# A gated linear attention and a maxout feed-forward in one kernel: where the loads of spans 5 to 9 and three stores stand in SyncE's queue

## The chip, the cores and the metric

The kernel runs on one core of one Trainium2 chip. The metric is the device time of one execution in microseconds (us); lower is better. The engines are TensorE (PE, with its weight loads as PEld), VectorE (DVE), ScalarE (ACT), GpSimd (POOL) and SyncE (SP). In this kernel SP does nothing but issue DMA transfers.

## What is computed

Inputs are `q`, `k`, `v` and `f_logit`, each 4 x 8 x 768 x 48 (batch, head, position, head dimension), and three weight matrices, all in float32. The first part is a gated recurrence for each batch and head:

```python
f = 1.0 / (1.0 + np.exp(-f_logit))
for t in range(S):
    state = f[:, :, t, :, None] * state + np.einsum('bhd,bhe->bhde', k[:, :, t], v[:, :, t])
    y[:, :, t] = np.einsum('bhd,bhde->bhe', q[:, :, t], state)
```

The second part takes the result as 3072 tokens of 384 values and puts them through a feed-forward of width 1024:

```python
h1 = x @ w1
h2 = x @ w2
g = np.maximum(h1, h2)
return (g @ w_out).astype(np.float32)
```

The output is 3072 x 384 in float32.

## The kernel before

**Tiling.** A *span* is 256 positions of one batch with all eight heads. There are 12 spans, numbered so that span s is window s // 4 of batch s % 4: spans 0 to 3 are the first windows of the four batches, spans 4 to 7 the second, spans 8 to 11 the third. The state that span s leaves is what span s + 4 begins with. Within a span two neighbouring positions share a partition, so that a tensor of a span is 128 partitions x 768 values, 384 KB.

**An order written out by hand.** The scheduler is switched off (`tc.manual_schedule()`). The string `ORDER` is a list of words, and the loop at the end of the kernel runs one step for each word. Each engine does its own steps in the order of the words; between engines only data dependencies count (and one added rule, below). A word has a letter for the step, the span (and sometimes a part), a letter for the engine (`a` ACT, `v` DVE, `p` POOL, `s` SP) and, behind `@`, a slot or a PSUM bank. The words that matter here:

- `Lf6@12`, `Lq`, `Lk`, `Lv`: SP loads one tensor of span 6 into slot 12 of `slots`, 27 slots of 384 KB in SBUF (line 126, `load`). A slot is used again later, so a load may have to wait for the last reader of what lay there. Slots 0 to 11 first hold the raw weights, 12 to 15 an intermediate of the weights.
- `E`, `F`, `G` (ACT): the gate from `f`, its logarithm, and one factor from that. `e` (DVE or POOL) adds two neighbouring positions, `C` (PE) sums over positions, `X` and `Z` (ACT) are the exponentials of the sums.
- `i` (POOL or DVE, line 248) multiplies `k` by a factor, in place in the slot; `j` (DVE, line 252) does the same to `q`. `K` (line 259) and `Q` (line 262) scale them into the tiles `kp` and `qp`, and `V` casts `v` into `vb`.
- `t` and `u` (PE, line 276) transpose `kp` and `qp` into PSUM, `U` copies the result to SBUF (`trs`).
- `A` (PE, line 293) forms the products of positions, `m` (DVE, line 300) masks them, `D` (PE, line 388) forms what a span adds to the state, `n` and `N` update the state. `S` and `y` (PE, lines 315 and 324) add up the attention output; `z` (DVE, lines 356 and 358) reads a column of the output's banks between the two halves `S.0` and `S.1`, so that the second half waits for it.
- `Y` copies the output to SBUF. For spans 6 to 10 it goes on through `M` (SP, line 428), a DMA transpose; for those spans the tile `xr` between `Y` and `M` has one buffer.
- `d` (PE, line 437) multiplies by `w1 - w2`, `r` takes the positive part, `o` (PE, line 462) multiplies by `w_out` and by the product `w2 @ w_out`, which together give the maximum. `b` copies an output block to `ob`, which has three buffers (spans 0, 3, 6, 9 share one, and so on), and `O` (SP, line 483 for most spans) stores it to HBM.

The feed-forward of a span stands some spans behind its attention in the list, so that PE has matrix products of `d` and `o` between the short steps of the attention.

**An added rule.** A POOL step among `e`, `i`, `K`, `Q`, `V`, `N` and some of the weights' steps also waits for the DVE step of that set that stands last before it in the list:

```python
        if key in SHARED and e in ("v", "p"):
            ins = nc.cur_bb.bb.instructions[-1]
            if e == "v":
                ahead = ins.name
            elif ahead:
                tc.add_manual_dep(ins, ahead, ...
```

**SP's queue.** SP issues one transfer after the other. A transfer whose slot is not free, or whose `ob` is not written, holds up all that stand behind it. Eight semaphores serve the transfers in turn, so that a transfer also waits for the one eight places ahead of it.

Of the kernel before, what the change touches and what calls it, by code (L numbers as in the profile page):

```python
# [17 lines left out]


ORDER = """  # L20
Lf0s@16 g0v Lf1s@17 Lq0s@18 Lk0s@19 Lk1s@20 Lv0s@21 Lq1s@22 Wa2s E0 Wb1s F0 Lv1s@23 E1 e0v C0@0 F1
Wb2s j0v Z0 e1v X0 Q0v G0 C1@1 Wb0s i0v X1 u0@2 G1 g2v K0v Lf2s@24 i1p t0@2 U0.0v@2 U0.1a@3 Wa0s V0v
Z1 K1v D0@2 A0.1@0 Wa3s j1v A0.0@4 Q1v Wa1s m0.1v@0 u1@6 t1@6 Wo0s n0.0v U1.0a@6 U1.1a@7 Wo1s V1v
n0.1v D1@0 m0.0v@4 S0.0@2 A1.0@6 Lk2s@25 wc2a z0v@2 m1.0v@6 A1.1@4 S0.1 y0 Lq2s@26 wc0a ws2p n1.0v
n1.1v m1.1v@4 S1.0@6 Y0.0a@2 wt2@0 Lf3s@16 E2 g5p z1v@6 N1.1v S1.1 y1 N0.1p Lv2s@17 g3p ws0v wt0@1
Y1.1a@7 wx2a@0 Y0.1v@3 wc1p Lq3s@18 Y1.0v@6 d0.2@2 F2 g1p ws3v d0.0@4 Lk3s@19 wx0a@1 wt1@0 g4v e2v
d0.3@3 ws1v C2@1 r0.1a@2 d1.2@6 Lf4s@21 wo0v wx1v@0 wo1p d0.1@5 G2 d1.3@7 r0.0v@4 d1.0@2 Lv3s@20
wo2p wo3a d1.1@3 r1.1v@6 Z2 wm0@0 X2 g6v Lk4s@22 r1.0a@2 i2v wm1@1 K2v Lf5s@23 j2v wm2@2 Q2v Lq4s@24
E3 wn1v@1 t2@4 u2@4 F3 U2.0v@4 Lf6s@12 V2p wn2a@2 wn0v@0 o0.1@1 U2.1v@5 e3p A2.1@2 Lq5s@13 b0.1.0a@1
D2@4 A2.0@6 G3 n2.0v C3@0 j3v o1.1@1 Z3 n2.1v Lk5s@0 i3v X3 Q3v o1.0@0 m2.1v@2 E4 K3p F4 m2.0v@6  # L30
b1.1.0a@1 S2.0@2 V3p u3@4 z2v@2 t3@4 e4p S2.1 y2 U3.2v@4 D3@6 Y2.2a@2 C4@1 n3.0v N2.1v A3.0@4 G4
n3.1v A3.1@2 m3.0v@4 E5 o0.0@6 i4p F5 m3.1v@2 Z4 d2.2@4 X4 e5v G5 j4v S3.0@2 b0.0.0a@6 d2.3@5 K4v E6
O0.2s C5@1 Lq6s@1 d2.1@7 z3v@2 r2.1a@4 Q4v Lv4s@2 S3.1 y3 Lk6s@3 F6 j5v Lf7s@4 N3.1v t4@4 X5 Y3.2v@2
i5p u4@4 Lv6s@5 Z5 d2.0@6 U4.2v@4 e6p d3.1@3 r2.0a@6 d3.0@2 g7p K5v G6 C6@1 d3.2@4 r3.0a@2 Q5v
d3.3@5 Z6 j6v X6 t5@2 u5@2 Q6v r3.1a@4 o2.1@1 U5.2v@2 V4a i6p b1.0.0a@0 O1.2s A4.1@2 K6p D4@4
m4.1v@2 A4.0@6 Lv5s@6 E7 o3.1@0 Lf8s@7 F7 Lq7s@8 n4.0v m4.0v@6 Lf9s@9 N4.0p e7p Lq9s@10 t6@2
b3.1.0a@0 u6@2 Lk7s@11 n4.1v G7 A5.0@6 U6.2v@2 S4.0@4 b2.1.0a@1 o3.0@0 m5.0v@6 V5p C7@1 z4v@4
b3.0.0v@0 A5.1@2 X7 A6.0@6 S4.1 y4 m5.1v@2 Z7 E8 D5@0 Y4.2v@4 V6a o2.0@2 F8 m6.0v@6 d4.2@4 n5.0v
b2.0.0a@2 N5.0v G8 d4.3@5 O2.2s n5.1v j7v Lq8s@25 S5.0@0 r4.1a@4 A6.1@2 N4.1v Lf11s@26 D6@6 z5v@0
Q7p S5.1 y5 Lv7s@14 n6.0v E9 m6.1v@2 Lk8s@15 d4.0@4 Y5.2a@0 Lv8s@16 d4.1@5 e8p Lf10s@17 F9 Lv9s@18  # L40
d5.1@1 r4.0v@4 i7p Lk9s@21 d5.0@0 o4.1@2 j8v r5.0a@0 N6.0v K7v n6.1v C8@3 e9v d5.2@0 Z8 b4.1.0v@2 G9
S6.0@4 u7@6 X8 t7@6 z6v@4 j9v S6.1 y6 V7v d5.3@1 U7.2v@6 i8p o4.0@2 r5.1a@0 Y6.2v@4 Q8p E11 M6s
A7.0@0 b4.0.0v@2 A7.1@4 D7@6 N5.1p m7.0v@0 o5.0@3 Lq11s@19 K8p Lk11s@20 n7.0v O3.2s m7.1v@4 C9@2
N7.0p b5.0.0a@3 t8@0 Z9 u8@0 N6.1v S7.0@4 V8v X9 o5.1@3 U8.2v@0 V9a F11 n7.1v i9v D8@2 b5.1.0a@3
A8.1@0 z7v@4 N7.1p A8.0@6 n8.0v E10 m8.1v@0 d6.2@2 K9p d6.3@3 m8.0v@6 d6.0@0 r6.1a@2 N8.0p d6.1@1
Q9v S8.0@2 r6.0a@0 S7.1 y7 z8v@2 j11v t9@6 u9@6 e11v Y7.2a@4 S8.1 y8 U9.2v@6 C11@0 G11 M7s o6.1@1
F10 i11p Z11 Lk10s@23 X11 Q11p o6.0@4 Y8.2a@2 e10p A9.0@6 b6.0.0a@4 D9@0 M8s A9.1@2 K11p n9.0v
d7.1@5 m9.1v@2 C10@0 O5.2s d7.0@4 Z10 m9.0v@6 Lq10s@22 b6.1.0a@1 d7.3@3 Lv11s@12 G10 d7.2@2 O4.2s
r7.0a@4 N9.0v i10p Lv10s@24 d8.3@7 O6.2s X10 d8.1@5 r7.1a@2 K10v d8.2@6 d8.0@4 r8.1a@6 o7.1@1
r8.0a@4 j10v Q10p S9.0@2 t11@4 t10@6 z9v@2 u11@4 S9.1 y9 U11.0v@4 u10@6 U11.1v@5 o7.0@0 U10.2a@6  # L50
V11v V10v b7.1.0v@1 o8.1@4 Y9.2a@2 b7.0.0a@0 M9s D10@1 b8.1.0a@4 D11@0 O7.2s A11.0@2 A10.0@6 n11.0v
A11.1@4 m10.0v@6 o8.0@0 m11.1v@4 d9.0@6 N11.0v n10.0v d9.1@7 m11.0v@2 N10.0p d9.3@5 r9.0a@6 d9.2@4
b8.0.0v@0 O8.2s S10.0@0 r9.1a@4 S11.0@2 z10v@0 A10.1@6 z11v@2 S11.1 y11 m10.1v@6 S10.1 y10 Y11.0a@2
Y11.1a@3 o9.0@4 Y10.2a@0 M10s d11.2@5 b9.0.0v@4 d11.1@0 d11.3@1 o9.1@4 d10.1@3 b9.1.0v@4 r11.4a@5
d10.0@2 O9.2s d10.2@4 r10.0a@2 d10.3@5 d11.0@2 r10.1v@4 o10.0@3 r11.2a@2 r11.3v@0 r11.5v@1 o10.1@0
b10.0.0a@3 o11.0@1 b10.1.0v@0 O10.2s o11.1@0 b11.0.0v@1 O11.0s o11.2@1 b11.1.1a@0 O11.1s b11.1.2a@1
O11.2s
"""


# [523 lines left out]
```

## Time and profile before

| | |
|---|---|
| three runs | 139.15, 140.23, 140.26 us, median 140.23 us |
| the profiled execution's own time | 141.28 us |
| its span, first to last instruction | 139.5 us |
| loaded from and stored to HBM in it | 23.59 MB and 4.72 MB |
| DMA of under 512 bytes a packet | 54368 of 59768 packets |
| one load of 384 KB, issue to landing, median | 6.1 to 6.5 us |
| one store of 384 KB, issue to landing, median | 4.6 us |

The profile tells the busy time of each engine, which engine or transfer ended each idle time, and when each transfer was issued and had landed. A matmul is pipelined, so that its shown duration includes time in which the next one already runs: the start of a group against the start of the next one tells how long PE had it. A wait for several things is put down to the one that came last, and where the engine that is named had long been done, it was another, often a DMA.

### The profile page before, as it was taken

Reading aid. Unit: us, or ns where it says so; the run is one execution under the profiler, and the core shown is the slowest. Engines: PE = TensorE matmul, PEld = TensorE weight load, DVE = VectorE, ACT = ScalarE, POOL = GpSimd, SP = SyncE. Lnnn points to the kernel's source line nnn. Section 1 sums busy time; section 2 is a strip of 40 time slices with the busy share of each in tenths; the row PEclk is TensorE's granted clock in tenths of the full one; section 3 lists DMA queues with packets and bytes.
Section 4 is the critical chain, followed back from the end, with each engine's and each line's share of the span. In section 5 each row is a group of like instructions: output and inputs, shape, how many; then the busy total and the mean of one; then the engine's idle time right before and its main releaser. Section 6 shows DMA issues by size and latency. Waiting matters only on the chain. (4 is left out here: it accounts for less than half of the span.)

```text
span 139.5 us, 5553 instructions
## 1 busy us (share of the span) xinstructions
PE 119.7 (86%) x2455; PEld 89.9 (64%) x2455; DVE 100.9 (72%) x173; ACT 79.0 (57%) x120; POOL 43.6 (31%) x52
## 2 busy tenths in 40 slices
PE   0044489699999989999999899989989999999991
PEld 0024378586567678667787666766877668778671
DVE  5688798999889989979985989981742768312630
ACT  3684257865583979853884356695565814504301
POOL 5002008540509206094055095629525001000000
PEclk9999999999999999999999999999999999999999
DMA  4999999999999889999999999909699061422124
GB/s 104 271 261 294 344 339 348 370 272 246 270 264 241 222 234 260 251 303 244 247 265 262 224 275 180 297 5 146 170 257 329 16 140 34 117 56 60 58 61 165
DMA packets 59768, 29.65 MB, mean 213 GB/s; under 512 B 54368, under 2 KB 58592, under 8 KB 59744
## 3 DMA queue, kind: packets, MB, share of 16 engines
q1 hardware_dynamic: 59744, 29.30, 85.0%
q8 instruction: 19, 0.31, 1.0%
q14 instruction: 5, 0.04, 0.1%
HBM read 23.59 MB, written 4.72 MB: 203 GB/s over the span
## 5 line engine op out<-in xcount | busy, mean ns | idle before, releaser
L437 PE MATMUL banks<-xT,wd 128*128 128x256 bf16 x288 | 34.6, 273 | 1.6 <-DVE xT L115 1.1
L462 PE MATMUL banks<-wo,gT 128*128 128x384 bf16 (+1 forms) x200 | 35.3, 320 | 0.0
L437 PEld LDWEIGHTS <-wd 128*128 128x128 bf16 x288 | 27.2, 98 | 6.0 <-POOL state L180 1.2
L446 ACT ACTIVATE gT<-banks 128x1024 bf16<-128x1024 f32 (+1 forms) x20 | 19.5, 981 | 18.2 <-PE banks L437 13.6
L300 DVE TENSOR_TENSOR at_m<-banks,mask 128x1024 bf16<-128x1024 f32 x24 | 28.8, 1216 | 0.8 <-PE banks L293 0.5
L462 PEld LDWEIGHTS <-gT 128*128 128x128 bf16 x200 | 19.2, 98 | 11.8
L248 POOL TENSOR_TENSOR slots<-slots,one 128x384 f32<-128x384 f32 x8 | 8.0, 999 | 29.5 <-DVE kp L259 8.6
L462 PE MATMUL banks<-m,xT 128*128 128x384 bf16 (+1 forms) x75 | 15.9, 320 | 0.0
L214 ACT ACTIVATE gate<-slots 128x768 f32<-128x768 f32 x12 | 10.1, 841 | 7.0 <-DMA slots<-in_f_logit_dram 6.0
L115 ACT COPY ob<-banks 128x384 f32<-128x384 f32 (+1 forms) x16 | 7.3, 457 | 11.8 <-PE banks L462 11.8
L115 DVE COPY trs<-banks 128x2048 bf16<-128x2048 bf16 (+1 forms) x12 | 11.9, 996 | 2.5 <-PE banks L276 2.5
L115 DVE COPY ob<-banks 128x384 f32<-128x384 f32 x9 | 5.0, 554 | 8.9 <-PE banks L462 8.9
L229 PE MATMUL banks<-e,u_inc 128*128 128x384 bf16 x12 | 4.2, 353 | 8.2 <-DVE e L225 8.1
L405 DVE TENSOR_TENSOR tmp_s<-banks,state 128x192 f32<-128x192 f32 x16 | 5.6, 352 | 7.0 <-PE banks L388 6.4
L218 ACT ACTIVATE ell<-gate 128x768 f32<-128x768 f32 x12 | 10.2, 847 | 0.2
L259 POOL TENSOR_TENSOR kp<-slots,inv 128x768 bf16<-128x768 f32 x5 | 9.1, 1817 | 3.8 <-DVE qp L262 3.7
L293 PE MATMUL banks<-trs 48*64 48x128 bf16 x384 | 10.1, 234 | 0.2
L262 POOL TENSOR_TENSOR qp<-slots,dec 128x768 bf16<-128x768 f32 x4 | 7.3, 1814 | 8.9 <-PE banks L388 6.2
L252 DVE SCALAR_TENSOR_TENSOR slots<-gate,slots 128x384 f32<-128x384 f32 x12 | 6.6, 551 | 3.0 <-DMA slots<-in_q_dram 3.0
L115 ACT COPY trs<-banks 128x1024 bf16<-128x1024 bf16 (+1 forms) x4 | 4.8, 1227 | 7.0 <-PE banks L276 7.0
L293 PEld LDWEIGHTS <-trs 48*64 48x64 bf16 x384 | 7.5, 115 | 1.7 <-issue 1.1
L462 PEld LDWEIGHTS <-xT 128*128 128x128 bf16 x75 | 6.5, 97 | 3.2
(73 smaller groups left out, 185.9 us busy)
## 6 DMA issues: line engine op xcount, KB each, us to landing
slots<-in_f_logit_dram SPq DMA_DIRECT2D x12, 384.0 KB, 6.5
slots<-in_q_dram SPq DMA_DIRECT2D x12, 384.0 KB, 6.1
slots<-in_k_dram SPq DMA_DIRECT2D x12, 384.0 KB, 6.3
slots<-in_v_dram SPq DMA_DIRECT2D x12, 384.0 KB, 6.1
out_dram<-ob SPq DMA_DIRECT2D x6, 384.0 KB, 4.6
out_dram<-ob SPq DMA_DIRECT2D x11, 192.0 KB, 3.5
slots<-in_moe_w_dram SPq DMA_DIRECT2D x4, 384.0 KB, 8.7
slots<-in_moe_w_dram SPq DMA_DIRECT2D x3, 512.0 KB, 8.7
```

Source lines behind the costliest of these rows:

```text
L115: (nc.scalar.copy if e == "a" else engines[e].tensor_copy)(out, in_)
L214: nc.scalar.activation(flat(gate[s]), flat(loaded[s]["f"]), AF.Exp, bias=0.0, scale=-1.0)
L218: nc.scalar.activation(flat(ell[s]), flat(gate[s]), AF.Ln, bias=1.0, scale=1.0)
L248: engines[e].tensor_mul(even, even, one[s])
L252: engines[e].scalar_tensor_tensor(out=even, in0=gate[s][:, :, 1, :], scalar=1.0, in1=even, op0=ALU.add, op1=ALU.mult)
L259: engines[e].tensor_mul(pad("kp", s)[:, :, :, 0:D], by_parity(loaded[s]["k"]), both(inv[s]))
L262: engines[e].tensor_mul(pad("qp", s)[:, :, :, 0:D], by_parity(loaded[s]["q"]), both(dec[s][:, 0:HD].rearrange("p (h d) -> p h d", h=H)))
L293: nc.tensor.matmul(out=ps[h * HC:(h + 1) * HC, j % 2, par, :], lhsT=t[rows, h, 0, j, par, :], rhs=t[rows, h, 1, j].rearrange("p a t -> p ( ...
L300: nc.vector.tensor_mul(at[s][:, jj].rearrange("p r j a t -> p (r j) (a t)"), banks[:, b:b + 2, :].rearrange("p r (j x) -> p (r j) x", j=2) ...
L437: nc.tensor.matmul(out=ps[:, f], lhsT=wd[:, kt, ff * C:(ff + 1) * C], rhs=xT[g][:, kt], start=(kt == 0), stop=(kt == KT - 1))
L446: nc.scalar.activation(dst, src, AF.Relu)
L462: nc.tensor.matmul(out=ps, lhsT=lhs, rhs=rhs, start=(i == 0), stop=(i == len(terms) - 1))
```

## The change

Only the string `ORDER` changes. All words are kept, with their slots and banks, and all words that are not for SP stand in the same order as before. On SP 17 words take other places among the transfers 32 to 49 (counted from 0). The lists of SP in that stretch, before and after; the transfers ahead of them and behind them are the same:

```diff
 Lk5@0
-O0.2 Lq6@1 Lv4@2 Lk6@3 Lf7@4 Lv6@5 O1.2 Lv5@6 Lf8@7
-Lq7@8 Lf9@9 Lq9@10 Lk7@11 O2.2 Lq8@25 Lf11@26 Lv7@14 Lk8@15
+Lq6@1 Lv4@2 Lk6@3 Lf7@4 O0.2 Lv5@6 Lf8@7 Lv6@5 Lq7@8
+O1.2 Lf9@9 Lk7@11 Lq8@25 Lv7@14 Lq9@10 Lk8@15 O2.2 Lf11@26
 Lv8@16
```

`O0.2` goes behind four loads, `O1.2` behind three others (`Lv5`, `Lf8`, `Lq7`), and `O2.2` behind `Lq8`, `Lv7` and `Lk8`. Among the loads, `Lv6` goes behind `Lv5` and `Lf8`; `Lk7`, `Lq8` and `Lv7` go ahead of `Lq9`; `Lv7` and `Lk8` go ahead of `Lf11`. From `Lv8` on every transfer has its old place.

More of the change, by code (lines that the diff above doesn't have):

```diff
@@ L20 @@
 ORDER = """
[L21 to L54, printed above, removed]
@@ L55 @@
-d10.0@2 O9.2s d10.2@4 r10.0a@2 d10.3@5 d11.0@2 r10.1v@4 o10.0@3 r11.2a@2 r11.3v@0 r11.5v@1 o10.1@0
-b10.0.0a@3 o11.0@1 b10.1.0v@0 O10.2s o11.1@0 b11.0.0v@1 O11.0s o11.2@1 b11.1.1a@0 O11.1s b11.1.2a@1
-O11.2s
+Lf0s@16 g0v Lf1s@17 Lq0s@18 Lk0s@19 Lk1s@20 Lv0s@21 Lq1s@22 Wa2s E0 Wb1s F0 Lv1s@23 E1 e0v C0@0 F1 Wb2s
+j0v Z0 e1v X0 Q0v G0 C1@1 Wb0s i0v X1 u0@2 G1 g2v K0v Lf2s@24 i1p t0@2 U0.0v@2 U0.1a@3 Wa0s V0v Z1 K1v
+D0@2 A0.1@0 Wa3s j1v A0.0@4 Q1v Wa1s m0.1v@0 u1@6 t1@6 Wo0s n0.0v U1.0a@6 U1.1a@7 Wo1s V1v n0.1v D1@0
@@ new lines @@
+m0.0v@4 S0.0@2 A1.0@6 Lk2s@25 wc2a z0v@2 m1.0v@6 A1.1@4 S0.1 y0 Lq2s@26 wc0a ws2p n1.0v n1.1v m1.1v@4
+S1.0@6 Y0.0a@2 wt2@0 Lf3s@16 E2 g5p z1v@6 N1.1v S1.1 y1 N0.1p Lv2s@17 g3p ws0v wt0@1 Y1.1a@7 wx2a@0
+Y0.1v@3 wc1p Lq3s@18 Y1.0v@6 d0.2@2 F2 g1p ws3v d0.0@4 Lk3s@19 wx0a@1 wt1@0 g4v e2v d0.3@3 ws1v C2@1
+r0.1a@2 d1.2@6 Lf4s@21 wo0v wx1v@0 wo1p d0.1@5 G2 d1.3@7 r0.0v@4 d1.0@2 Lv3s@20 wo2p wo3a d1.1@3 r1.1v@6
+Z2 wm0@0 X2 g6v Lk4s@22 r1.0a@2 i2v wm1@1 K2v Lf5s@23 j2v wm2@2 Q2v Lq4s@24 E3 wn1v@1 t2@4 u2@4 F3
@@ new lines @@
+U2.0v@4 Lf6s@12 V2p wn2a@2 wn0v@0 o0.1@1 U2.1v@5 e3p A2.1@2 Lq5s@13 b0.1.0a@1 D2@4 A2.0@6 G3 n2.0v C3@0
+j3v o1.1@1 Z3 n2.1v Lk5s@0 i3v X3 Q3v o1.0@0 m2.1v@2 E4 K3p F4 m2.0v@6 b1.1.0a@1 S2.0@2 V3p u3@4 z2v@2
+t3@4 e4p S2.1 y2 U3.2v@4 D3@6 Y2.2a@2 C4@1 n3.0v N2.1v A3.0@4 G4 n3.1v A3.1@2 m3.0v@4 E5 o0.0@6 i4p F5
+m3.1v@2 Z4 d2.2@4 X4 e5v G5 j4v S3.0@2 b0.0.0a@6 d2.3@5 K4v E6 C5@1 Lq6s@1 d2.1@7 z3v@2 r2.1a@4 Q4v
+Lv4s@2 S3.1 y3 Lk6s@3 F6 j5v Lf7s@4 O0.2s N3.1v t4@4 X5 Y3.2v@2 i5p u4@4 Z5 d2.0@6 U4.2v@4 e6p d3.1@3
@@ new lines @@
+r2.0a@6 d3.0@2 g7p K5v G6 C6@1 d3.2@4 r3.0a@2 Q5v d3.3@5 Z6 j6v X6 t5@2 u5@2 Q6v r3.1a@4 o2.1@1 U5.2v@2
+V4a i6p b1.0.0a@0 A4.1@2 K6p D4@4 m4.1v@2 A4.0@6 Lv5s@6 E7 o3.1@0 Lf8s@7 Lv6s@5 F7 Lq7s@8 O1.2s n4.0v
+m4.0v@6 Lf9s@9 N4.0p e7p t6@2 b3.1.0a@0 u6@2 Lk7s@11 Lq8s@25 Lv7s@14 Lq9s@10 Lk8s@15 n4.1v G7 A5.0@6
+U6.2v@2 S4.0@4 b2.1.0a@1 o3.0@0 m5.0v@6 V5p C7@1 z4v@4 b3.0.0v@0 A5.1@2 X7 A6.0@6 S4.1 y4 m5.1v@2 Z7 E8
+D5@0 Y4.2v@4 V6a o2.0@2 F8 m6.0v@6 d4.2@4 n5.0v b2.0.0a@2 N5.0v G8 d4.3@5 O2.2s n5.1v j7v S5.0@0 r4.1a@4
@@ new lines @@
+A6.1@2 N4.1v Lf11s@26 D6@6 z5v@0 Q7p S5.1 y5 n6.0v E9 m6.1v@2 d4.0@4 Y5.2a@0 Lv8s@16 d4.1@5 e8p Lf10s@17
+F9 Lv9s@18 d5.1@1 r4.0v@4 i7p Lk9s@21 d5.0@0 o4.1@2 j8v r5.0a@0 N6.0v K7v n6.1v C8@3 e9v d5.2@0 Z8
+b4.1.0v@2 G9 S6.0@4 u7@6 X8 t7@6 z6v@4 j9v S6.1 y6 V7v d5.3@1 U7.2v@6 i8p o4.0@2 r5.1a@0 Y6.2v@4 Q8p E11
+M6s A7.0@0 b4.0.0v@2 A7.1@4 D7@6 N5.1p m7.0v@0 o5.0@3 Lq11s@19 K8p Lk11s@20 n7.0v O3.2s m7.1v@4 C9@2
+N7.0p b5.0.0a@3 t8@0 Z9 u8@0 N6.1v S7.0@4 V8v X9 o5.1@3 U8.2v@0 V9a F11 n7.1v i9v D8@2 b5.1.0a@3 A8.1@0
@@ new lines @@
+z7v@4 N7.1p A8.0@6 n8.0v E10 m8.1v@0 d6.2@2 K9p d6.3@3 m8.0v@6 d6.0@0 r6.1a@2 N8.0p d6.1@1 Q9v S8.0@2
+r6.0a@0 S7.1 y7 z8v@2 j11v t9@6 u9@6 e11v Y7.2a@4 S8.1 y8 U9.2v@6 C11@0 G11 M7s o6.1@1 F10 i11p Z11
+Lk10s@23 X11 Q11p o6.0@4 Y8.2a@2 e10p A9.0@6 b6.0.0a@4 D9@0 M8s A9.1@2 K11p n9.0v d7.1@5 m9.1v@2 C10@0
+O5.2s d7.0@4 Z10 m9.0v@6 Lq10s@22 b6.1.0a@1 d7.3@3 Lv11s@12 G10 d7.2@2 O4.2s r7.0a@4 N9.0v i10p Lv10s@24
+d8.3@7 O6.2s X10 d8.1@5 r7.1a@2 K10v d8.2@6 d8.0@4 r8.1a@6 o7.1@1 r8.0a@4 j10v Q10p S9.0@2 t11@4 t10@6
@@ new lines @@
+z9v@2 u11@4 S9.1 y9 U11.0v@4 u10@6 U11.1v@5 o7.0@0 U10.2a@6 V11v V10v b7.1.0v@1 o8.1@4 Y9.2a@2 b7.0.0a@0
+M9s D10@1 b8.1.0a@4 D11@0 O7.2s A11.0@2 A10.0@6 n11.0v A11.1@4 m10.0v@6 o8.0@0 m11.1v@4 d9.0@6 N11.0v
+n10.0v d9.1@7 m11.0v@2 N10.0p d9.3@5 r9.0a@6 d9.2@4 b8.0.0v@0 O8.2s S10.0@0 r9.1a@4 S11.0@2 z10v@0
+A10.1@6 z11v@2 S11.1 y11 m10.1v@6 S10.1 y10 Y11.0a@2 Y11.1a@3 o9.0@4 Y10.2a@0 M10s d11.2@5 b9.0.0v@4
+d11.1@0 d11.3@1 o9.1@4 d10.1@3 b9.1.0v@4 r11.4a@5 d10.0@2 O9.2s d10.2@4 r10.0a@2 d10.3@5 d11.0@2
@@ L58 @@
+r10.1v@4 o10.0@3 r11.2a@2 r11.3v@0 r11.5v@1 o10.1@0 b10.0.0a@3 o11.0@1 b10.1.0v@0 O10.2s o11.1@0
+b11.0.0v@1 O11.0s o11.2@1 b11.1.1a@0 O11.1s b11.1.2a@1 O11.2s
 """
```

## The prediction

> **What bounds the kernel now.** I read the page first, then the stretches of 5 us, then the chain that ended last.
>
> ```profile
> span 139.5 us, 5553 instructions
> ...
> PE 119.7 (86%) x2455; PEld 89.9 (64%) x2455; DVE 100.9 (72%) x173; ACT 79.0 (57%) x120; POOL 43.6 (31%) x52
> ```
>
> The profiled execution took 141.28 us by its own time, 1.78 us more than its span; the median of the three runs shown is 140.23 us. I make the sum against 141.28 and take the difference over to the median. PE is the busiest engine. The table of stretches has, after the times, PE, PEld, DVE, ACT and POOL with their instructions, the granted clock, the DMA share and GB/s:
>
> ```profile
> 70.00:75.00 5.00, 5.00 (x151) 4.38 (x150) 3.76 (x7) 3.54 (x5) 3.59 (x3) 1.00 1.06 275
> 75.00:80.00 5.00, 4.55 (x106) 3.23 (x105) 4.03 (x11) 2.31 (x4) 0.15 (x1) 1.00 0.95 224
> ```
>
> In the first PE is busy throughout, at full clock; in the second 0.45 us are missing, and DMA carries 224 GB/s instead of 275. Behind 88 us the chain of waits is nearly all PE, of which this is the beginning and the one transfer in it:
>
> ```profile
> 88.86 2.78 PE banks L437 x24
> ...
> 97.89 4.37 DMA xT<-xr
> ```
>
> PE's list is fixed. So time is won only where PE now waits, and a wait that ends sooner moves what follows as one block. The transfer in the chain, the transpose `M8`, is released by PE's own output of span 8 (`y8`, then `Y8`), so it moves along. The question is which waits of PE the moved transfers end, directly or through DVE and POOL.
>
> **What SP gains.** SP's waits for `ob` at line 483 (total, times, longest), and some of its issues (start, duration):
>
> ```profile
> SPq L483 <- ACT ob L115: 4.8, 3, 2.2
> ```
>
> ```profile
> 49.37 0.48 SPq L483 DMA_DIRECT2D out_dram<-ob  x1
> ```
>
> ```profile
> 66.27 1.33 SPq L126 DMA_DIRECT2D slots<-in_k_dram  x1
> 69.85 0.36 SPq L483 DMA_DIRECT2D out_dram<-ob  x1
> 70.30 0.39 SPq L126 DMA_DIRECT2D slots<-in_q_dram  x1
> 70.77 0.69 SPq L126 DMA_DIRECT2D slots<-in_f_logit_dram  x1
> ```
>
> SP stood at `O0`, `O1` and `O2` for 4.8 us until ACT had written `ob`. Each is reached three or four loads later now, when its block is written (`O0`'s at 49.37, `O2`'s at 69.85), so SP no longer stops there. Little of the 4.8 us comes back as bandwidth, as loads issued earlier keep DMA at work meanwhile (the share above is 0.95 even in the stretch behind `O2`). What changes for certain is the order of landing. I bound it by places, counted from 0 along the queue: a load lands about when the transfer at its new place landed before. Time from issue to landing (min, median, max), first for `Lv4` and `Lk6`, issued at 50.4 and 51.6, then for `Lk7`, `Lq8` and `Lf11`, issued at 66.27, 70.30 and 70.77:
>
> ```profile
> DMA to landing us min/median/max: 6.9/7.2/7.6
> ```
>
> ```profile
> DMA to landing us min/median/max: 5.8/6.3/6.6
> ```
>
> By the first, place 34 (`Lv4`) landed at 50.4 + 6.9 = 57.3 and place 35 (`Lk6`) at 51.6 + 7.6 = 59.2. By the second, with 6.3, 5.8 and 6.6 in that order, place 44 landed at 72.6, place 46 at 76.1 and place 47 at 77.4. After the change these places hold `Lk6` (57.3 instead of 59.2), `Lq8` (72.6 instead of 76.1), `Lq9` (76.1, later than before) and `Lk8` (77.4).
>
> **Term 1, `Lk6` to PE's `t6`.** POOL, PE and DVE at that place:
>
> ```profile
> 59.37 1.00 POOL L248 TENSOR_TENSOR slots<-slots,one 128x384 f32<-128x384 f32 x1 [4.01 <-DVE trs L115]
> 60.45 1.82 POOL L259 TENSOR_TENSOR kp<-slots,inv 128x768 bf16<-128x768 f32 x1
> ```
>
> ```profile
> 60.18 0.66 PE L462 MATMUL banks<-m,xT 128*128 128x384 bf16 x3
> 60.67 1.46 PE L462 MATMUL banks<-wo,gT 128*128 128x384 bf16 x8
> 62.33 0.41 PE L276 MATMUL banks<-ident,kp 64*128 64x64 bf16 x16 [0.19 <-POOL kp L259]
> 62.57 0.40 PE L276 MATMUL banks<-ident,qp 64*128 64x64 bf16 x16
> ```
>
> ```profile
> 57.18 0.96 DVE L262 TENSOR_TENSOR qp<-slots,dec 128x768 bf16<-128x768 f32 x1
> ```
>
> The first row is `i6`. Its wait is put down to a DVE copy that it does not read; what it reads is `Lk6`, landed at 59.2. `K6` then runs to 62.27, and PE's `t6` starts at 62.33, having waited. With `Lk6` at 57.3, `i6` is held next by the added rule, until `Q6` on DVE ends at 58.14. So `i6` starts near 58.2, `K6` ends near 61.1, and PE is last at `t6`. When would PE be there? Three matmuls of `o` hold it for 0.49 us, start to start, 0.163 each, so the eight from 60.67 on hold it until 61.98: `t6` waited 0.35 us. The row says 0.19, as its ends of matmuls include the pipeline's tail. I take 0.35.
>
> **Term 2, `Lq8` through DVE to PE's `S6.1`.**
>
> ```profile
> 73.89 1.22 DVE L448 TENSOR_SCALAR gT<-banks 128x1024 bf16<-128x1024 f32 x1 [0.96 <-PE banks L437]
> 76.08 0.56 DVE L252 SCALAR_TENSOR_TENSOR slots<-gate,slots 128x384 f32<-128x384 f32 x1 [0.97 <-DMA slots<-in_q_dram]
> ...
> 78.90 0.15 DVE L356 COPY look<-banks 128x2 f32<-128x2 f32 x1
> 78.97 0.55 DVE L252 SCALAR_TENSOR_TENSOR slots<-gate,slots 128x384 f32<-128x384 f32 x1
> 79.43 0.55 DVE L115 CAST vb<-slots 128x768 bf16<-128x768 f32 x1
> ```
>
> ```profile
> 77.73 0.27 PE L324 MATMUL banks<-state,trs 48*128 48x48 bf16 x8
> 77.84 0.65 PE L276 MATMUL banks<-ident,qp 64*128 64x64 bf16 x16
> 78.32 0.41 PE L276 MATMUL banks<-ident,kp 64*128 64x64 bf16 x16
> 79.10 0.27 PE L324 MATMUL banks<-state,trs 48*128 48x48 bf16 x8 [0.38 <-DVE look L356]
> ```
>
> `j8` stood 0.97 us at DVE's head until `Lq8` landed, and from there DVE ran without a gap to `z6` (78.90 to 79.05), for which PE's `S6.1` waited. With `Lq8` at 72.6, `j8` follows the step that ends at 75.11, and `z6` waits only for `S6.0`, which ends at 78.00. Then PE is last: `t7` began at 78.32 and holds PE for 0.24 us (as `t6` did, 62.33 to 62.57), so `S6.1` could start at 78.56 instead of 79.10: 0.54 us.
>
> **Term 3, `Lk8` through POOL to PE's `t8`.**
>
> ```profile
> 80.28 1.00 POOL L248 TENSOR_TENSOR slots<-slots,one 128x384 f32<-128x384 f32 x1 [5.13 <-DMA slots<-in_k_dram]
> ```
>
> ```profile
> 83.48 1.82 POOL L259 TENSOR_TENSOR kp<-slots,inv 128x768 bf16<-128x768 f32 x1
> ```
>
> ```profile
> 85.03 0.24 PE L232 MATMUL banks<-ones,e 128*128 128x2 bf16 x4
> 85.35 0.41 PE L276 MATMUL banks<-ident,kp 64*128 64x64 bf16 x16
> ```
>
> `i8` waited for `Lk8`. With that at 77.4 the added rule holds it until DVE's `V7` (79.43 to 79.98 now) is done, which comes sooner by `z6`'s 0.9 us and term 1, 1.2 us together. `K8` (83.48 to 85.30) moves with it, and PE is last at `t8`: 85.27 to 85.35, 0.1 us.
>
> Sum: 0.35 + 0.54 + 0.1 = 1.0 us, as each moves PE's block. The bounds: 0.19 + 0.38 = 0.57 if only the idle times that the rows name go; 0.35 + 1.25 = 1.6 if PE follows DVE's whole lead at `S6.1` (`j8` from 76.08 to 75.11, 0.97, and POOL's 0.3 behind it). What lands later I cost at nothing: `Lv6` and `Lf11`; `Lq9` (76.1), as `j9` began at 78.97 and would begin near 77.7, with 1.6 us left; and `O0`, whose `ob` is written again by `b3`. `O0` is at place 36 now, where `Lf7` landed for ACT's `E7`, and `b3` is two steps behind that on ACT:
>
> ```profile
> 60.70 0.84 ACT L214 ACTIVATE gate<-slots 128x768 f32<-128x768 f32 x1 [1.83 <-DMA slots<-in_f_logit_dram]
> ```
>
> ```profile
> 62.33 0.46 ACT L115 COPY ob<-banks 128x384 f32<-128x384 f32 x1
> ```
>
> From 60.7 to 62.33 1.6 us are left; if that cover were gone, ACT would stand there, and PE's `o3.0` behind it. The forecast is 141.28 - 1.0 = 140.3 for the profiled execution and 140.23 - 1.0 = 139.2 for the median.
>
> **A rule that speaks against it.** By the first row of stretches PE is busy 5.00 of 5 us. The Trainium skill (Perfetto Trace Analysis, Identifying the Most-Contended Engine) says that matmul occupancy is a poor measure of how near PE is to its limit, as matmuls are pipelined, and that the share of time in weight loads is a better one. By that share (64% on the page) PE would have a third of its time free, could soak up the lead, and the time would stay. I weigh against it that 24 matmuls of `d` follow each other in 2.78 us, 0.116 each, without a wait, which the share does not tell. The case stands first among the rivals.
>
> **The rivals.** *Lead lost* (0.13): PE has room in its list, or the wait of 4.37 us for `M8` takes the lead back. For it: that is idle time of PE in the chain. Against it: `M8` is released by PE's own output. Time: 0 to 0.5 us less than now, 139.7 to 140.2. *More than the three waits* (0.25): DVE is 72% busy and full at these places; 1.2 us ahead, it frees other steps that share PE's short waits, and part of the 4.8 us comes back as earlier landings of all behind `Lv8`. Time: 1.4 to 2.2 us less, about 138.5. *`Lq9` too late* (0.09, slower): it moves behind `Lk7`, `Lq8` and `Lv7`. If it lands behind 78.97, DVE stands at `j9`, and `V7`, `U7` and PE's `A7` come later than now. From about 71.2 for its old landing (one load ahead of 72.6) this needs three loads at over 2.6 us each; 384 KB at 275 and 224 GB/s take 1.43 and 1.76. At 3.2 us a load it lands at 80.8, 1.8 us behind 78.97, and the time is 142.0. That the change doesn't do what it says is no case here: it is SP's list itself.
>
> **The numbers.** The forecast has 0.53, *lead lost* 0.13, *more* 0.25, *too late* 0.09. About 1% is what can be told from no change (the three runs of before spread by 0.8%): 138.83 and 141.63. *More* lies nearly all below 138.83, the forecast in part, by its upper bound: faster 0.24 + 0.10 = 0.34. Slower is *too late*, 0.09; the rest, 0.57, is within 1%. The range takes in the forecast's bounds (138.6 to 139.7), *lead lost* up to 140.3, and the nearer part of *more*, down to 138.1.
>
> **What would show it.** Right: SP issues `O0`, `O1` and `O2` without standing; `i6` starts near 58.2 and `t6` no longer waits for `kp`; `j8` starts near 74.8 without a wait for its load and `S6.1` at 77.9 to 78.2 without one for `look`; POOL's wait of 5.13 us is shorter; the block of `d` at 88.86 starts 1.0 us sooner. Wrong: a wait of DVE for `in_q` at `j9`, of ACT or DVE for a store before an `ob` copy, or idle time of PE behind 88 us that grew by what was won.

## The result, and the profile after

The changed kernel takes 138.96 us in the median of 22 runs, against 140.01 us for the kernel before in 22 runs: a ratio of 0.9933 with a 95% interval of 0.9908 to 0.9957, or 1.05 us less. The forecast for the median was 139.2 us, 1.0 us less. The profiled execution of the changed kernel took 138.83 us by its own time.

The page of the changed kernel, span and busy times of the engines:

```profile
span 137.1 us, 5554 instructions
...
PE 119.2 (87%) x2455; PEld 90.1 (66%) x2455; DVE 100.3 (73%) x173; ACT 78.9 (58%) x120; POOL 43.7 (32%) x52
```

Its stretches of 5 us, with the columns of before (PE, PEld, DVE, ACT, POOL, granted clock, DMA share, GB/s):

```profile
70.00:75.00 5.00, 4.73 (x123) 4.04 (x124) 3.45 (x7) 3.42 (x5) 3.74 (x3) 1.00 1.14 295
75.00:80.00 5.00, 5.00 (x112) 3.73 (x111) 4.88 (x10) 2.67 (x6) 1.49 (x2) 1.00 1.17 278
```

The work of each engine is the same as before. In 75 to 80 us PE now lacks nothing, where it lacked 0.45 us, and DMA moves 278 GB/s instead of 224. In 70 to 75 us PE lacks 0.27 us that it did not lack before; that comes up again below. The source of the changed kernel is two lines shorter, so its line numbers are lower by two throughout: L481 here is L483 of the prediction. In the experiments the numbers are those of before.

SP no longer stands at these three stores. Its issues around `O2` (start, duration):

```profile
69.48 1.37 SPq L124 DMA_DIRECT2D slots<-in_k_dram  x1
70.94 1.24 SPq L481 DMA_DIRECT2D out_dram<-ob  x1
72.28 1.12 SPq L124 DMA_DIRECT2D slots<-in_f_logit_dram  x1
```

`O2` goes out 0.09 us behind the load ahead of it; before, 2.25 us passed between the end of one (66.27 + 1.33) and the start of the other (69.85). `O0` and `O1` (53.99 and 60.81) go out 0.10 us behind the load ahead of them. POOL and DVE at the places of the three terms:

```profile
57.38 1.01 POOL L246 TENSOR_TENSOR slots<-slots,one 128x384 f32<-128x384 f32 x1 [2.86 <-DVE qp L260]
58.47 1.82 POOL L257 TENSOR_TENSOR kp<-slots,inv 128x768 bf16<-128x768 f32 x1
...
78.51 1.00 POOL L246 TENSOR_TENSOR slots<-slots,one 128x384 f32<-128x384 f32 x1 [4.52 <-DVE vb L113]
```

```profile
73.14 1.23 DVE L446 TENSOR_SCALAR gT<-banks 128x1024 bf16<-128x1024 f32 x1 [0.84 <-PE banks L435]
74.28 0.55 DVE L250 SCALAR_TENSOR_TENSOR slots<-gate,slots 128x384 f32<-128x384 f32 x1
...
77.29 0.16 DVE L354 COPY look<-banks 128x2 f32<-128x2 f32 x1
77.36 0.55 DVE L250 SCALAR_TENSOR_TENSOR slots<-gate,slots 128x384 f32<-128x384 f32 x1
```

`i6` (first row) and `i8` (third) are now released by `Q6` and `V7` on DVE, as the added rule has it, not by a load. `j8` (74.28) follows the step ahead of it without a wait, and so does `j9` (77.36), whose load was moved back. PE at the same places, `t6`, then `u7`, `t7` and `S6.1`, then the end of `C9` and `t8`:

```profile
61.23 0.41 PE L274 MATMUL banks<-ident,kp 64*128 64x64 bf16 x16
...
77.09 0.39 PE L274 MATMUL banks<-ident,qp 64*128 64x64 bf16 x16
77.32 0.40 PE L274 MATMUL banks<-ident,kp 64*128 64x64 bf16 x16
77.55 0.26 PE L322 MATMUL banks<-state,trs 48*128 48x48 bf16 x8
...
83.47 0.24 PE L230 MATMUL banks<-ones,e 128*128 128x2 bf16 x4
83.65 0.41 PE L274 MATMUL banks<-ident,kp 64*128 64x64 bf16 x16
```

None of them has an idle time before it. From `t7` to `S6.1` it is 0.23 us, where it was 0.78.

The two spans shown differ by 2.46 us, the medians by 1.05. Of the 2.46 us, 0.74 lie ahead of `C6` on PE (54.98 against 54.23), 0.96 between `C6` and `d6.2` (88.86 against 87.15), where the moved transfers can act, and 0.75 behind that. One execution of each kernel is not enough here, which is why both were profiled again.

### The profile page after: what moved, and what is told of

Same layout as the page of the kernel before. It is cut to its first block, busy times and chain, and to the rows that moved or that the text cites. A ratio compares the mean times of both kernels' runs of the same rounds, so it can differ in the third digit from the quotient of the medians.

```text
span 137.1 us, 5554 instructions
## 1 busy us (share of the span) xinstructions
PE 119.2 (87%) x2455; PEld 90.1 (66%) x2455; DVE 100.3 (73%) x173; ACT 78.9 (58%) x120; POOL 43.7 (32%) x52
## 4 chain that ended last, share of the span: by engine, by line
PE 65%; DMA 11%; SPq 9%; DVE 6%; ACT 5%; issue 2%; DVEq 0%; ACTq 0%
PE banks L460 29%; PE banks L435 18%; DMA slots<-in_moe_w_dram 8%; SPq L124 6%; PE banks L313 4%; DMA xT<-xr 3%; PE banks L274 3%; PE banks L502 3%; PE banks L291 3%; PE banks L322 3%; SPq L139 2%; PE banks L386 1%; DVE qp L260 1%; ACT ell L216 1%; DVE trs L113 1%
## 5 line engine op out<-in xcount | busy, mean ns | idle before, releaser
L446 DVE TENSOR_SCALAR gT<-banks 128x1024 bf16<-128x1024 f32 (+1 forms) x6 | 6.0, 1042 | 3.3 <-PE banks L435 3.3
```

## The experiments

Two theories stood against each other. *Three waits*: a moved load counts through the wait of PE that it ends, and the order of landing decides. *Bandwidth*: what pays is SP's 4.8 us, which come back as earlier landings of everything. Each kernel below is the kernel before or the changed one with other places in SP's queue and nothing else. Where an expectation quotes landing times from the changed kernel's profile (74.2, 78.1, 79.6, 72.9), they were counted from a wrong zero and are 0.3 to 0.4 us too late.

**The first part alone.**

```diff
-O0.2 Lq6 Lv4 Lk6 Lf7
+Lq6 Lv4 Lk6 Lf7 O0.2
```

> The kernel before with one move: O0 goes behind Lq6, Lv4, Lk6 and Lf7; everything from Lv6 on keeps its place, so SP still stands at O1 and O2. By the theory of three waits (a load counts through the wait of PE that it ends) only term 1 comes: i6 starts by 58.5 in the time scale of before, PE's t6 is no longer put down to kp and starts 0.2 to 0.35 us sooner against the step ahead of it, S6.1 still waits for look behind j8; total 0.2 to 0.4 us less than before, a ratio of 0.997 to 0.9986. By the rival that the returned bandwidth of SP's 4.8 us is what pays, SP saves only about 0.9 us at O0, a fifth of it, and the total falls by about 0.2 us, but with t6 waiting as before and the gain spread over later waits.

139.75 us, a ratio of 0.9964 (0.9933 to 0.9996). `t6` starts 1.89 us behind the step ahead of it, `o3.1`, as in the changed kernel, and is not put down to `kp`.

**The third part alone.**

```diff
-Lq9 Lk7 O2.2 Lq8 Lf11 Lv7 Lk8
+Lk7 Lq8 Lv7 Lq9 Lk8 O2.2 Lf11
```

> The kernel before with the transfers 43 to 49 in the new order (Lk7, Lq8, Lv7, Lq9, Lk8, O2, Lf11); O0 and O1 stay ahead, SP stands there as before. By the theory of three waits terms 2 and 3 come without term 1: t6 waits for kp as before, j8 has no wait for its load, S6.1 none for look and is 0.5 to 0.6 us nearer to the step ahead of it, t8 0.1 us; total 0.6 to 0.8 us less, a ratio of 0.994 to 0.996. By the rival of bandwidth SP saves only its 2.2 us at O2, about half of 4.8, and the total falls by half of the whole change's 0.93 us, 0.4 to 0.5 us.

139.12 us, a ratio of 0.9941 (0.9906 to 0.9975). `S6.1` and `t8` do not wait; `t6` waits as before, 2.29 us behind `o3.1`.

**The loads alone, and the stores late with the three loads at their old places.** The first keeps `O0`, `O1` and `O2` where they were; the second takes `Lk6`, `Lq8` and `Lk8` back to places 35, 46 and 49 of the changed list.

```diff
-O0.2 Lq6 Lv4 Lk6 Lf7 Lv6 O1.2 Lv5 Lf8 Lq7 Lf9 Lq9 Lk7 O2.2 Lq8 Lf11 Lv7 Lk8
+O0.2 Lq6 Lv4 Lk6 Lf7 Lv5 O1.2 Lf8 Lv6 Lq7 Lf9 Lk7 Lq8 O2.2 Lv7 Lq9 Lk8 Lf11
```

> The loads in the new order, but O0, O1 and O2 at their old places 32, 38 and 45, so that SP stands at each of them as before. By the theory of three waits the order of the loads is what counts: Lq8 is at place 44, ahead of O2, and j8 has no wait, S6.1 none for look; Lk6 keeps place 35, and t6 waits as before; Lk8 is at place 48 instead of 49 and i8 gains little. Total 0.5 to 0.6 us less than before, a ratio of about 0.996. By the rival of bandwidth nothing is won, as SP stands for the same 4.8 us: ratio 1.000, with j8 at 76 as before or another wait in its place.

```diff
-Lq6 Lv4 Lk6 Lf7 O0.2 Lv5 Lf8 Lv6 Lq7 O1.2 Lf9 Lk7 Lq8 Lv7 Lq9 Lk8 O2.2 Lf11
+Lq6 Lv4 Lf7 Lk6 O0.2 Lv5 Lf8 Lv6 Lq7 O1.2 Lf9 Lk7 Lv7 Lq9 Lq8 Lf11 O2.2 Lk8
```

> The stores late as in the changed kernel, so that SP does not stand, but the three loads that the terms name at their old places: Lk6 at 35 (behind Lf7), Lq8 at 46 and Lk8 at 49. By the theory that the place in the order is what counts the gain is gone: Lk6 lands near 59, i6 and K6 as before, Lq8 near 76 and j8 waits, ratio 0.998 to 1.000. By the rival of bandwidth the gain stays: with SP not standing, place 46 landed at 74.2 in the changed kernel's profile, where j8 started at 74.28, so j8 does not wait; Lk6 lands near 59 and K6 ends at 60.9 against 61.1 for PE; Lk8 lands near 78.1, ahead of the end of V7; ratio 0.993 to 0.994, as with the whole change.

139.25 us, 0.9928 (0.9894 to 0.9962), and 138.72 us, 0.9910 (0.9872 to 0.9947). So neither theory holds alone: the order pays while SP stands as before, against *bandwidth*, and the earlier landings pay with the order taken back, against *three waits* as I had put it. In both PE waits at `t6`, first in the loads alone, then with the old places:

```profile
62.15 0.41 PE L276 MATMUL banks<-ident,kp 64*128 64x64 bf16 x16 [0.90 <-POOL kp L259]
```

```profile
62.59 0.41 PE L276 MATMUL banks<-ident,kp 64*128 64x64 bf16 x16 [0.90 <-POOL kp L259]
```

In both `Lk6` is at place 35 and lands at 59.1 and 59.5. Up to `Lf7`, the transfer behind `Lk6`, the queue of the loads alone is that of the kernel before, so that its wait at `t6` is one more value of the wait there, and a long one. In neither does `S6.1` wait. With the old places that is in part owed to the wait at `t6`: `Lq8` landed at 74.87 and `j8` started at 75.29, about 1 us later than it could have without that wait. Without it `j8` would, by an estimate from these three times, have waited about 0.6 us for `Lq8`. In the loads alone `Lq8` landed at 72.69, 2.2 us ahead of `j8`, so that the order alone is enough there.

**One load late.** Two kernels take one load back in the changed list: `Lq8` to place 49, `Lq9` to place 50.

```diff
-Lk7 Lq8 Lv7 Lq9 Lk8 O2.2 Lf11 Lv8
+Lk7 Lv7 Lq9 Lk8 O2.2 Lf11 Lq8 Lv8
```

> The changed kernel with Lq8 alone moved back, behind Lf11, to place 49. By the theory that DVE's wait for Lq8 passes through z6 to PE's S6.1: Lq8 lands near 78 (place 49 landed at 78.1 in the changed kernel's profile), j8 starts near 78.2 instead of 74.28, DVE's steps to z6 follow without a gap, S6.1 is put down to look and starts near 81.3 instead of 77.55, and the total is 3.3 to 3.9 us above the changed kernel's, about 142.5 us, a ratio of 1.016 to 1.020 to the kernel before. By the rival that DVE and PE have room in their lists to soak up such a wait (PE with its weight loads at two thirds of the time) the total rises by less than 1 us, a ratio below 1.001.

143.03 us, a ratio of 1.0212 (1.0173 to 1.0251), 4 us over the changed kernel and just above what was expected. Its `j8` and `z6` on DVE and what PE has next of span 6 and 7:

```profile
77.35 0.56 DVE L252 SCALAR_TENSOR_TENSOR slots<-gate,slots 128x384 f32<-128x384 f32 x1 [3.56 <-DMA slots<-in_q_dram]
...
80.16 0.15 DVE L356 COPY look<-banks 128x2 f32<-128x2 f32 x1
```

```profile
78.23 0.27 PE L324 MATMUL banks<-state,trs 48*128 48x48 bf16 x8 [1.76 <-DVE state L410]
78.33 0.19 PE L276 MATMUL banks<-ident,qp 64*128 64x64 bf16 x1
79.37 0.55 PE L276 MATMUL banks<-ident,qp 64*128 64x64 bf16 x15 [0.85 <-DVE tmp_s L405]
```

`j8` starts 3.07 us later than in the changed kernel (77.35 against 74.28), and PE waits, but not where I had it: first for `N6.0` at `S6.0` (1.76 us), then in the middle of `u7` for `n6.1` (0.85 us), both behind `j8` on DVE. The second of these waits was there in the kernel before too. Behind them PE runs 2.8 us late: `S6.1` starts at 80.37, in the changed kernel at 77.55. It could not start sooner, as `z6`, which stands behind `j8` on DVE, ended at 80.31. The rest of the 4 us comes from `S6.1` to `A7.0`, without any wait. The stretches of 5 us of this kernel (columns as above, the granted clock third from the end):

```profile
75.00:80.00 5.00, 2.39 (x50) 1.80 (x50) 2.65 (x6) 1.29 (x3) 0.00 (x0) 0.94 1.00 243
80.00:85.00 5.00, 4.98 (x101) 3.41 (x98) 3.56 (x7) 1.75 (x2) 3.62 (x4) 0.72 0.50 115
85.00:90.00 5.00, 5.00 (x115) 3.33 (x104) 5.00 (x9) 2.60 (x5) 1.90 (x2) 1.00 1.09 192
```

PE stood for 2.61 us of the first stretch, and its granted clock fell to 0.94 and then 0.72. `S6.1` to `A7.0` (80.37 to 84.58) take 4.21 us, in the changed kernel 3.14 (77.55 to 80.69) at full clock: 1.07 us more. So the wait passed on makes 2.8 us and the lower clock 1.1. The clock was already low for the last 0.9 us ahead of `S6.1`, but PE would have waited for `z6` there. No theory had the lower clock.

```diff
-Lk7 Lq8 Lv7 Lq9 Lk8 O2.2 Lf11 Lv8
+Lk7 Lq8 Lv7 Lk8 O2.2 Lf11 Lv8 Lq9
```

> The changed kernel with Lq9 alone moved back, behind Lv8, to place 50: the price of the rival that Lq9 comes too late. Place 50 landed at 79.6 in the changed kernel's profile, and j9 started at 77.36. If DVE's lateness passes on (V7, then POOL's i8, Q8 and K8 by the added rule, then PE's t8), the total rises by about as much as Lq9 is late, 1.8 to 2.3 us above the changed kernel's, near 141, a ratio of 1.005 to 1.010 to the kernel before. If only U7 and PE's A7 feel it, A7 starts about 1.1 us later and the total rises by 1.1. If lists have room, it rises by less than 0.5.

140.74 us, a ratio of 1.0046 (1.0011 to 1.0081), some 1.8 us over the changed kernel. Its `j9`, and PE's two halves of `A7` and `t8`:

```profile
79.36 0.56 DVE L252 SCALAR_TENSOR_TENSOR slots<-gate,slots 128x384 f32<-128x384 f32 x1 [2.26 <-DMA slots<-in_q_dram]
```

```profile
81.58 0.42 PE L293 MATMUL banks<-trs 48*64 48x128 bf16 x16 [1.16 <-DVE trs L115]
82.44 0.42 PE L293 MATMUL banks<-trs 48*64 48x128 bf16 x16 [0.45 <-DVE xr L115]
...
85.58 0.41 PE L276 MATMUL banks<-ident,kp 64*128 64x64 bf16 x16 [0.34 <-POOL kp L259]
```

A wait of 2.26 us becomes 1.16 + 0.45 + 0.34 = 1.95 us of PE's, by `U7`, by `Y6` and by `K8`. PE's list soaks up little at either place.

**Both kernels once more**, first profiled only, then timed too.

> The kernel before, unchanged, profiled once more. By the theory of three waits t6 waits for kp behind Lk6, j8 for Lq8, S6.1 for look, as in the first profile; the idle time of PE at S3.0 (0.57 us) and between u9 and S8.1 (0.73 us), which the profile of the changed kernel does not have, are the chance of one execution and are absent, smaller or elsewhere here. By the rival that the change ended these two as well, they are here again, at the same steps and of the same size.

139.96 us. The waits for `kp`, for the load at `j8` and for `look` are there again; those at `S3.0` and `S8.1` are smaller and gone. PE in this profile of the kernel before:

```profile
61.88 0.41 PE L276 MATMUL banks<-ident,kp 64*128 64x64 bf16 x16 [0.55 <-POOL kp L259]
...
77.63 0.40 PE L276 MATMUL banks<-ident,kp 64*128 64x64 bf16 x16
78.27 0.27 PE L324 MATMUL banks<-state,trs 48*128 48x48 bf16 x8 [0.24 <-DVE look L356]
...
84.20 0.24 PE L232 MATMUL banks<-ones,e 128*128 128x2 bf16 x4
84.74 0.41 PE L276 MATMUL banks<-ident,kp 64*128 64x64 bf16 x16 [0.30 <-POOL kp L259]
```

> The changed kernel, unchanged, profiled once more. By the theory of three waits t6 is not put down to kp, j8 has no wait for its load and S6.1 none for look, as in the first profile; PE's idle time at D6 (0.48 us) is the chance of one execution and is absent, smaller or elsewhere. If it is the change's own, it is here again.

139.40 us. None of the three waits is there. PE's idle time ahead of `D6` is there again, 0.34 us.

> The kernel before against itself: what the comparison gives for no change. Every theory expects a ratio of 1.000 within 0.0035, the half width of the other comparisons.

140.09 us beside 140.29 us for the same kernel: a ratio of 0.9962 (0.9931 to 0.9993), which leaves out 1. So a ratio here can be off by 0.004, and the ratios from 0.991 to 0.996 above are not to be ranked; the waits in their traces can be. This third profile of the kernel before shows where else `j8` counts:

```profile
77.12 0.19 PE L276 MATMUL banks<-ident,qp 64*128 64x64 bf16 x1
77.94 0.39 PE L276 MATMUL banks<-ident,qp 64*128 64x64 bf16 x15 [0.63 <-DVE tmp_s L405]
78.16 0.40 PE L276 MATMUL banks<-ident,kp 64*128 64x64 bf16 x16
78.94 0.27 PE L324 MATMUL banks<-state,trs 48*128 48x48 bf16 x8 [0.37 <-DVE look L356]
```

`u7` stops after its first transpose. Its second bank still holds what `n6.1` on DVE reads, and `n6.1` stands behind `j8`.

> The changed kernel once more, beside the stores alone on one chip. Every theory expects its first ratio again, 0.991 to 0.996. By the theory of three waits its profile has no wait of t6 for kp, of j8 for its load and of S6.1 for look; idle time of PE that the profile puts down to issue stands at other steps than in the first profile or is of another size there.

139.23 us, a ratio of 0.9954 (0.9908 to 1.0). No wait for the three loads, and idle time ahead of `D6` once more, 0.58 us.

**The stores alone**: the stores at their new places, all loads in the old order.

```diff
-O0.2 Lq6 Lv4 Lk6 Lf7 Lv6 O1.2 Lv5 Lf8 Lq7 Lf9 Lq9 Lk7 O2.2 Lq8 Lf11 Lv7 Lk8
+Lq6 Lv4 Lk6 Lf7 O0.2 Lv6 Lv5 Lf8 Lq7 O1.2 Lf9 Lq9 Lk7 Lq8 Lf11 Lv7 O2.2 Lk8
```

> O0, O1 and O2 at their new places, all loads in the old order. Lk6 is at place 34 as in the whole change, Lq8 at 45 (one later than there), Lk8 at 49 (two later). By the theory of three waits, with places read from the changed kernel's profile (45 landed at 72.9, 49 at 78.1), t6, S6.1 and t8 wait for none of the three loads, and the total is that of the whole change, 0.8 to 1.1 us less than before, a ratio of 0.992 to 0.9945; the order among the loads adds nothing to the later stores. By the rival that each part adds its own share, the stores alone give less than the whole change by what the order of the loads won alone (1.0 us), so nothing: ratio about 1.000.

139.67 us, a ratio of 0.9939 (0.9908 to 0.9970). `t6` and `S6.1` do not wait, but `t8` does, as `Lk8` comes last. Its `i8` on POOL, then `t8` on PE:

```profile
79.65 1.00 POOL L248 TENSOR_TENSOR slots<-slots,one 128x384 f32<-128x384 f32 x1 [5.09 <-DMA slots<-in_k_dram]
```

```profile
84.72 0.41 PE L276 MATMUL banks<-ident,kp 64*128 64x64 bf16 x16 [0.49 <-POOL kp L259]
```

So the ratio is as expected and the reason is not: my expectation that `t8` would be free of `Lk8` fell.

## Why the prediction was right

The same intervals in all profiles, worked out from starts on PE's timeline in us: from `o3.1` to `t6`, from `u7` to `S6.1`, from the second part of `C9` (its four small matmuls) to `t8`, from the last full matmul group ahead of `D6` (`A6.1`) to `D6`, and the whole stretch from `C6` to `d6.2` (54.98 to 88.86 in the first profile of before).

```
                        t6     S6.1   t8     D6     C6 to d6.2
before, 1st             2.15   1.26   0.32   0.22   33.88
before, 2nd             2.51   0.87   0.54   0.22   34.09
before, 3rd             1.89   1.81   0.34   0.22   34.14
changed, 1st            1.89   0.46   0.18   0.70   32.92
changed, 2nd            1.89   0.46   0.18   0.56   32.80
changed, 3rd            1.89   0.46   0.18   0.80   33.10
first part alone        1.89   1.03   0.51   0.23   33.65
third part alone        2.29   0.46   0.18   0.22   33.76
loads alone             2.86   0.46   0.18   0.22   33.55
old places              2.87   0.46   0.17   0.22   33.65
stores alone            1.90   0.46   0.73   0.22   33.63
```

The stretch takes 34.04 us on average before and 32.94 after: 1.10 us, which agrees with the 1.05 us of the medians within what these can tell. Outside the stretch the two kernels' executions overlap: ahead of `C6` 54.3 to 55.0 us before and 53.9 to 54.5 after, from `d6.2` to the span's end 49.8 to 51.5 before and 49.9 to 50.9 after. The three profiles of one kernel agree within 0.3 us in the stretch, while the executions as a whole scatter: those of before took 141.28, 139.96 and 141.97 us by their own time, those of the changed kernel 138.83, 139.40 and 139.43. That is why the stretch is compared.

- **Term 1, 0.35 us at `t6`: right in kind, 0.3 in size.** The three profiles of before have 0.26, 0.62 and 0 over the 1.89 us that the step takes when nothing holds it (I had 1.79 for that). It depends on when `Lk6` happens to land, at 57.9 to 59.2. The third part alone and the loads alone have the order of before up to `Lk6`, and the wait there is 0.40 and 0.97 us: over these five profiles 0.45 on average. In the old places it is 0.98. PE was no sooner in these two long waits: `o3.1` starts 5.11 and 5.20 us behind `C6`, before 5.10 to 5.20. What differs is the load: `Lk6` landed 4.90 and 5.00 us behind the start of `C6`, in the three profiles of before 3.33 to 4.54. So no lead was lost here; the wait grows with how late `Lk6` lands.
- **Term 2, 0.54 us at `S6.1`: the mechanism right, the size too small.** I took `look` as the one gate and left out that `u7` had stopped, too (0.65 us for 16 transposes in the row quoted, 0.39 after). From `u7` to `S6.1` PE had lost 0.80, 0.41 and 1.35 us over 0.46, 0.85 on average; without the third profile, whose execution was the longest, 0.6. Both waits hang on `j8`: it waited 0.97, 0.58 and 1.52 us in these profiles and 0.74 in the first part alone, and PE lost 0.17 us less each time (0.80, 0.41, 1.35 and 0.57). So PE follows nearly the whole wait of DVE, the case that the prediction had as its upper bound only. That `Lq8` sets them is shown by its late return, which made PE 2.8 us late at `S6.1`.
- **Term 3, 0.1 us at `t8`: right, 0.22 on average** (0.14, 0.36 and 0.16). The stores alone, where `Lk8` lands last, have it at 0.55.
- **What I did not forecast: 0.47 us given back ahead of `D6`**, in all three profiles of the changed kernel and in none of the other ten. Two of these ten, with `Lq8` and with `Lq9` late, have the changed order up to `Lk7`, so it isn't shown that the change brings this loss about. The terms come to 0.29 + 0.85 + 0.22 = 1.36, less 0.47 makes 0.89, and smaller differences in the stretch the rest of 1.10. So the sum of 1.0 was right with its largest part too small and one loss missing; that the two nearly cancel is luck.
- **"Little of the 4.8 us comes back as bandwidth" was the step that failed.** `Lv8`, whose place is the same, landed at 81.8, 81.0 and 81.5 before and at 79.2, 79.4 and 81.7 after, 1.3 us sooner on average, over a quarter of the 4.8 us, and up to 2.5 us, though the last of the six not at all. In the old places, where the three loads stand as before, `S6.1` and `t8` wait no more than in the changed kernel, `S6.1` with the help of the wait at `t6`. The order and the bandwidth end the same waits, and either is nearly enough for terms 2 and 3; only `t6` needs the order. Reading the places as bounds kept the forecast safe from this error.
- **What lands later cost nothing**, as forecast: `j9` has no wait, and no copy to `ob` waits for a store. The price named for `Lq9` was right: with 2.0 us of lateness at `j9` (79.36 against 77.36) the median is some 1.8 us longer.
- **The rule that spoke against it.** The Trainium skill (Perfetto Trace Analysis, Identifying the Most-Contended Engine) judges PE's headroom by the share of time in weight loads, beside the arithmetic that it does, and not by its busy time. By that share (64% on the page of before) PE had a third of its time free. The traces do not agree that this time could soak up a wait: `j8` 3.07 us later made PE 2.8 us late at `S6.1`, before the clock added its part, and a wait of 2.26 us at `j9` became about 1.8.

No run points to a list that beats the changed one: every part taken away leaves one of the three waits, and the stretch from `C6` to `d6.2` is shortest with all of them. By their medians alone the loads alone and the old places can't be told from the changed kernel.

## What to carry to other kernels

In a queue that is issued in order, a store that waits for its result belongs behind the loads that are ready; look up when the store's block is written and put it just behind that. A load matters through the first engine in whose list it is last: follow that engine's next steps, all of them, to where the bound engine waits, and expect a second wait behind the first. Profile both kernels several times and compare the stretch around the change; a total that scatters by 1% cannot show a gain of 0.3 us, the waits in the stretch can.

## What the runs showed beside it

The idle time that PE's rows put down to issue is not loose. The changed kernel's PE and PEld ahead of `D6`:

```profile
70.27 0.24 PE L291 MATMUL banks<-trs 48*64 48x128 bf16 x1 [0.30 <-issue]
```

```profile
70.27 0.10 PEld L291 LDWEIGHTS <-trs 48*64 48x64 bf16 x1 [0.47 <-issue]
```

It is always the 16th matmul of `A6.1` that stands, in three of three profiles. The trace has 19 instruction packets of 16384 bytes on queue 8, among those of the loads. Here is the packet ahead of three such places, with the time from its end to the start of the next step on PE:

```
                          packet          idle   next step   behind the packet
before, 1st, S3.0         46.94 to 47.88  0.57   49.23       1.34
changed, 1st, S3.0        45.38 to 46.53  0      48.73       2.20
changed, 1st, D6          67.55 to 68.77  0.48   70.28       1.51
changed, 3rd, D6          68.18 to 69.35  0.58   70.74       1.39
before, 1st, D6           67.28 to 69.00  0      70.96       1.96
before, 3rd, S8.1         90.93 to 91.98  1.08   93.58       1.60
changed, 1st, S8.1        87.80 to 88.98  0      90.94       1.96
```

In 13 profiles PE stands at one of these three places only if the step begins 1.3 to 1.6 us behind the end of a packet, and for up to 1.1 us. No such step begins sooner than that behind a packet, while five of the 39 begin within these times and stand for less than 0.05 us. In the six profiles of the two kernels the wait at `S8.1` is 0.7, 0 and 1.1 us before and 0, 0.9 and 0 after, and the time from `d6.2` to the span's end is 50.7, 49.8 and 51.5 us before and 49.9, 50.9 and 50.0 after: it goes with this wait. That fits PE reaching instructions that have not arrived, and it would explain both the scatter of the executions and the 0.47 us ahead of `D6`, where the changed kernel's PE comes sooner. It is an agreement of times; no run moved a packet, so the cause is argued and not shown.

The granted clock in the run with `Lq8` late was the second surprise. All four executions of that kernel had a mean clock of 0.988; every other profile shown has 0.998 or more. PE's idle time of 1.76 and 0.85 us, with only 0.3 us of work between them, was enough to lower it. What was lost, (0.06 + 0.28) times 5 us, or 1.7 us, is half the clock for 3.4 us. The stretches of 3.41 us show it (columns as above):

```profile
76.02:79.43 3.41, 0.80 (x19) 0.50 (x18) 2.08 (x5) 1.10 (x3) 0.00 (x0) 1.00 0.97 241
79.44:82.85 3.41, 3.39 (x78) 2.67 (x78) 3.41 (x7) 0.07 (x1) 1.47 (x2) 0.50 0.81 195
```

PE had worked for 0.80 of 3.41 us when the clock fell to 0.50. By the Trainium skill (TensorE: Matmul & The Clock Gate, Part 1: The HAM clock gate) the clock is halved after an idle window of about 3.4 us. The trace agrees with a half for such a time, not with the length of idle time that it takes: 2.61 us in two pieces did here. With `Lq9` late, whose waits were shorter, two of the ten executions had a mean clock of 0.988 too, and took 142.68 and 143.75 us against 140.41 to 141.68 for the other eight. These two were not profiled. Two waits of PE that come close together can therefore cost more than their length; whether the longer one alone would have done, no run shows.

The loads themselves also scatter: `Lk5`, at the same place behind the same transfers in all these kernels, landed between 51.2 and 52.8 us.
